# A gated mix of linear attention and a token-mixing MLP: the first loads in one queue

## The chip, the cores and the metric

One NeuronCore of a Trainium2 chip runs the whole kernel. The metric is the device time of one execution in microseconds (us), as the median of several runs; less is better. TensorE multiplies matrices (its weight loads are listed on their own, as PEld), VectorE (DVE) and ScalarE (ACT) work elementwise, GpSimd (POOL) has only some set-up here. Transfers are issued by an engine's queue, here SyncE's (SP) and in a few places ScalarE's (ACTq), and are carried out by 16 DMA engines.

## The reference

```python
def _B_ref(x, w1, b1, w2, b2):          # S=2048 tokens, D=512, F=1792
    h = _layernorm(x, axis=-1)
    u = jnp.einsum("bsd,sf->bdf", h, w1) + b1
    u = _gelu(u)
    y = jnp.einsum("bdf,fs->bds", u, w2) + b2
    return y.transpose(0, 2, 1)

def _A_ref(x, wqkv, wo):                # 32 heads of 16
    q, k, v = split(x @ wqkv)
    phi = lambda t: jnp.where(t > 0, t + 1, jnp.exp(t)) + 1e-6
    pq, pk = phi(q), phi(k)
    kv = jnp.einsum("bhsd,bhse->bhde", pk, v);  z = pk.sum(over tokens)
    o = (pq @ kv) / (pq . z + 1e-6)
    return o @ wo

g = _sigmoid((x * gate_w).sum(-1, keepdims=True))
out = g * _A_ref(x, ...) + (1 - g) * _B_ref(x, ...)
```

(Shapes and reshapes are shortened.) Two paths read the same x: linear attention, and an MLP that mixes over tokens, so that its first product sums over all 2048 tokens. A gate per token mixes the two.

## The kernel before

Tokens are cut into 16 tiles of 128 (t), D into 4 blocks, F into 14 blocks of 128 (j or f). TensorE's work stands in the program's order, in these stages:

1. 18 warm-up matmuls on constants (`warm_ps`).
2. `accA`: the first 8 blocks of u. For t = 0 to 11 all eight blocks are fed from token tile t (`mlp1(accA[j], w1A, j * P, t, ...)`), so the matmuls go t by t, eight at a time; the last four tiles go block by block, each followed by its gelu. A matmul of tile t needs `xh[:, t, :]`, the normalised tile, and block j of `w1A[:, t, :]`.
3. `kacc` and `Gps`: phi(k), and the product of pk with x.
4. `accB`, the last 6 blocks of u, mixed with `kvps`, `w2ps` and `qacc` (q and phi(q)).
5. `yps`: for each token tile 14 matmuls over f (`w2h` with `uT`) and 4 over attention (`pqT` with `W2sb`), in groups of tiles 0-7, 8-11, 12-14 and 15. In a group all f products come first, and the attention products of its tiles after them.

The layernorm of a tile is VectorE's and ScalarE's work: VectorE takes the statistics of x tile t (L195, tiles 1 and 3 in two halves), aggregates them (L198), ScalarE takes the square root (`sd`, L200), VectorE the reciprocal (L206) and applies it (`xh`, L208). VectorE runs its instructions strictly in the order written, which is: statistics and aggregate of tile 0, the first half of tile 1's statistics, reciprocal and `xh` of tile 0, the second half of tile 1, its aggregate, `xh` of tile 1, statistics of tile 2, and so on. At tile 8 it also turns `b_rows`, the bias rows, into columns (L234 to L236).

Transfers are issued by the helper `load` (L123), on SP unless another queue is named; every one of them has line 124 in the profile. `pin` keeps the written order. Before the change ScalarE's queue issues two of the first loads: b1's rows and the first 128 columns of w1's row tile 0 (L134, L135). SP issues x tile 0, x tile 1, the other 896 columns of w1's row tile 0, row tile 1, x tiles 2 and 3, and from there x tile t+1 and w1 row tile t in turn, b2's rows behind row tile 4 (L138 to L148). Then come the gate's row, wk, the 16 transposing loads of x, w1's last 768 columns (`w1B`), wv, wo and wq. Each transfer signals its end on one of eight semaphores, used in turn over both queues; a transfer is issued only when the one eight places before it has landed.

Late in the kernel SP also carries `w2`: its first half into the buffer of `w1A`, its second half into that of `w1B`, which comes free when the last accB matmul has run. The second half is issued in pieces (`pieces`, L508) between the stores of the normalised q tiles to DRAM (L414) and the transposing loads that bring them back as `pqT` (L416).

Of the kernel before, what the change touches and what calls it, by code (L numbers as in the profile page):

```python
# [15 lines left out]
def kernel(  # L16
# [13 lines left out]
    nc = tc.nc  # L30
    P = nc.NUM_PARTITIONS
# [11 lines left out]
    NF = F // P  # L43
# [4 lines left out]
    FA = NFA * P  # L48
# [5 lines left out]
    w1_view = B_w1.rearrange("(t p) f -> p t f", p=P)  # L54
    w2_view = B_w2.rearrange("(f p) s -> p f s", p=P)
    b1_view = B_b1.rearrange("(f p) -> f p", p=P)
# [9 lines left out]
    def ptile(shape, dt, name):  # L66
        return persist.tile(shape, dt, name=name, tag=name)
# [27 lines left out]
    b_rows = ptile([32, P], BF16, "b_rows")  # L95
# [22 lines left out]
    w1A = wpool.tile([P, NT, FA], BF16, name="w1A", tag="w1st")  # L118
# [4 lines left out]
    def load(o, i, eng=None, **kw):  # L123
        pin((eng or nc.sync).dma_start(out=o, in_=i, **kw))  # L124

    def load_x(t0, t1):
        load(xr[:, t0:t1, :], x_view[:, t0:t1, :])

    def load_w1a(t):
        load(w1A[:, t, :], w1_view[:, t, 0:FA])  # L130


    tbl = work.tile([P, 1], FP32, name="tbl", tag="tbl", bufs=2)
    load(b_rows[0:NF, :], b1_view, nc.scalar)  # L134
    load(w1A[:, 0, 0:P], w1_view[:, 0, 0:P], nc.scalar)  # L135
    pin(nc.scalar.activation(out=tbl[:], in_=eps_t[:], func=ACT.Sqrt))

    load_x(0, 1)  # L138
    load_x(1, 2)
    load(w1A[:, 0, P:FA], w1_view[:, 0, P:FA])  # L140
    load_w1a(1)
    load_x(2, 3)
    for t in range(2, NT):
        if t + 1 < NT:
            load_x(t + 1, t + 2)
        load_w1a(t)
        if t == 4:
            load(b_rows[NF : NF + NT, :], b2_view)  # L148
    load(gw_b[:], gw_row_view.to_broadcast([P, D]))
    load(wk_sb[:], wqkv_view[:, :, D : 2 * D])  # L150
# [354 lines left out]

    pieces = {0: ((0, 4), (4, 7)), 5: ((7, 9),), 7: ((9, NF),)}  # L508
    for t in range(12):
        normalise(t)  # L510
        if t % 4 == 3:
# [83 lines left out]
```

## Time and profile before

| | us |
|---|---|
| median of 3 runs | 163.27 (162.86 to 163.67) |
| the profiled execution | 163.07 |
| its span, first to last instruction | 161.4 |
| TensorE matmul busy | 157.6 (98%) |
| VectorE busy | 118.7 (74%) |
| ScalarE busy | 53.1 (33%) |
| moved by DMA | 28.33 MB, 176 GB/s on the mean |

The span is the profiler's, and it is shorter than the execution's own time by what lies before the first and after the last instruction. A slice of the page's second part is a fortieth of the span, some 4 us. The chain of waits is followed back from the last instruction, at each step to what released it; shares in it are what set the end, while shares of busy time are not. In rows of instructions the columns are start, duration, engine, line, operation, output from inputs, shape, count, and in square brackets the idle time before it with what ended it. A duration of an SPq or ACTq row is the time that the queue takes to issue the transfer, not the transfer.

### The profile page before, as it was taken

To read this page: it belongs to the slowest core of one execution; us is meant where nothing else is said; L and a number is where in the kernel's file an instruction comes from. 1 tells how busy PE (TensorE), PEld (TensorE's weight loads), DVE (VectorE), ACT (ScalarE), POOL (GpSimd) and SP (SyncE) were. 2 spreads that over 40 slices of the span, in tenths; PEclk is the share of its full clock that TensorE was granted. 3 is DMA by queue.
4 is the path that set the end of the run, shared out by engine and by line. 5 is a ranking of instruction groups with operands and counts; after the bars stand their busy time and mean duration, and the time that the engine had idled before them with its cause. 6 is when DMAs were issued, how large, how long until landed. Compare 5 with 4: busy or idle time off the path is not lost.

```text
span 161.4 us, 2274 instructions
## 1 busy us (share of the span) xinstructions
PE 157.6 (98%) x820; PEld 73.1 (45%) x820; DVE 118.7 (74%) x278; ACT 53.1 (33%) x89; POOL 1.2 (1%) x8
## 2 busy tenths in 40 slices
PE   7999999999999999999999999999999999999993
PEld 5444444444444444444444444444444444444452
DVE  2799998959999998899895999999999970000002
ACT  4122227794342321434225970000008300550050
POOL 2000000000000000000000000000000000000000
PEclk9999999999999999999999999999999999999999
DMA  4999999444699630229952007826525935744421
GB/s 124 308 342 351 341 283 149 108 103 106 158 391 391 149 123 0 87 50 300 399 214 67 0 33 262 290 66 154 174 65 124 340 89 126 230 143 100 151 98 33
DMA packets 36838, 28.33 MB, mean 176 GB/s; under 512 B 20444, under 2 KB 31196, under 8 KB 36828
## 3 DMA queue, kind: packets, MB, share of 16 engines
q1 hardware_dynamic: 36384, 27.90, 57.6%
q10 hardware_dynamic: 444, 0.30, 0.6%
q8 instruction: 6, 0.10, 0.3%
q14 instruction: 4, 0.03, 0.0%
HBM read 19.28 MB, written 4.46 MB: 147 GB/s over the span
## 4 chain that ended last, share of the span: by engine, by line
PE 95%; DMA 2%; ACTq 0%; DVE 0%; issue 0%; DVEq 0%
PE yps L74 39%; PE accA L74 17%; PE accB L74 13%; PE qacc L74 9%; PE Gps L74 9%; PE kacc L74 9%; DMA w1A<-in_B_w_dram 2%; ACTq L124 0%; PE kvps L74 0%; DVE ot L539 0%; PE w2ps L74 0%; DVE b_rows L114 0%; DVEq L539 0%; DVE eps_t L115 0%
## 5 line engine op out<-in xcount | busy, mean ns | idle before, releaser
L74 PE MATMUL yps<-uT,w2h 128*128 128x512 bf16 (+2 forms) x238 | 49.2, 366 | 0.0
L74 PEld LDWEIGHTS <-w2h 128*128 128x128 bf16 x238 | 22.8, 98 | 25.9
L74 PE MATMUL accA<-xh,w1A 128*128 128x512 bf16 x128 | 28.0, 381 | 0.1
L532 ACT ACTIVATE ot<-yps,c,c 128x512 bf16<-128x512 f32 x15 | 11.6, 777 | 46.9 <-PE yps L74 34.8
L74 PE MATMUL accB<-xh,w1B 128*128 128x512 bf16 x96 | 21.5, 379 | 0.0
L539 DVE TENSOR_SCALAR ot<-yps,c,c 128x384 bf16<-128x384 f32 (+1 forms) x2 | 1.1, 542 | 25.5 <-PE yps L74 25.5
L74 PEld LDWEIGHTS <-w1A 128*128 128x128 bf16 x128 | 12.6, 98 | 15.6 <-DMA w1A<-in_B_w_dram 0.6
L74 PEld LDWEIGHTS <-xT 128*128 128x128 bf16 x128 | 12.3, 98 | 14.9 <-issue 0.2
L74 PE MATMUL Gps<-pk,xr 128*128 128x512 bf16 x64 | 15.8, 379 | 0.0
L74 PE MATMUL kacc<-wk_sb,xT 128*128 128x512 bf16 x64 | 15.8, 379 | 0.0
L74 PE MATMUL yps<-W2sb,pqT 128*128 128x512 bf16 (+2 forms) x68 | 14.6, 366 | 0.0
L74 PEld LDWEIGHTS <-w1B 128*128 128x128 bf16 x96 | 9.4, 98 | 11.3
L74 PE MATMUL qacc<-wq_sb,xT 128*128 128x512 bf16 x64 | 14.5, 379 | 0.0
L288 ACT ACTIVATE e<-qacc 128x512 bf16<-128x512 f32 x16 | 9.6, 597 | 12.2 <-DVE kvbdT L436 4.6
L288 ACT ACTIVATE e<-kacc 128x512 bf16<-128x512 f32 x16 | 9.2, 598 | 12.7 <-DVE pk L295 6.8
L290 DVE TENSOR_SCALAR e<-e 128x512 bf16<-128x512 bf16 x32 | 9.2, 288 | 4.6 <-ACT e L288 4.3
L195 DVE BATCH_NORM_STATS2 stats<-xr 128x6 f32<-128x512 bf16 (+1 forms) x18 | 10.9, 608 | 2.1 <-DMA xr<-in_A_x_dram 2.1
L408 DVE SCALAR_TENSOR_TENSOR pq<-pq,odds,rd 128x512 bf16<-128x512 bf16 x16 | 12.0, 752 | 0.6
L404 DVE TENSOR_REDUCE den<-prod 128x32 f32<-128x544 f32 x16 | 11.5, 720 | 0.6
L295 DVE SCALAR_TENSOR_TENSOR pk<-kacc,e 128x512 bf16<-128x512 f32 x16 | 11.1, 692 | 1.0
L295 DVE SCALAR_TENSOR_TENSOR pq<-qacc,e 128x512 bf16<-128x512 f32 x16 | 11.1, 692 | 0.6
L247 DVE CUSTOM_DVE_ANT_0 junk<-xr,gw_b 128x512 bf16<-128x512 bf16 x16 | 11.0, 690 | 0.5
(52 smaller groups left out, 95.5 us busy)
## 6 DMA issues: line engine op xcount, KB each, us to landing
w1A<-in_B_w_dram SPq DMA_DIRECT2D x15, 256.0 KB, 4.1
w2h<-in_B_w_dram SPq DMA_DIRECT2D x2, 1792.0 KB, 9.6
w1B<-in_B_w_dram SPq DMA_DIRECT2D x4, 768.0 KB, 7.6
xr<-in_A_x_dram SPq DMA_DIRECT2D x16, 128.0 KB, 4.0
q_dram<-pq SPq DMA_DIRECT2D x16, 128.0 KB, 3.4
out_dram<-ot SPq DMA_DIRECT2D x15, 128.0 KB, 1.9
w2h<-in_B_w_dram SPq DMA_DIRECT2D x1, 1280.0 KB, 6.7
w2h<-in_B_w_dram SPq DMA_DIRECT2D x1, 1024.0 KB, 5.1
```

Of the source, the lines that this page charges most:

```text
L74: nc.tensor.matmul(o, lhsT=lhsT, rhs=rhs, start=start, stop=stop, **kw)
L195: pin(nc.vector.bn_stats(out=stats[t][:, h, :], in_=xr[:, t, d0:d1]))
L247: nc.vector.tensor_tensor_reduce(out=junk[:], in0=xr[:, t, :], in1=gw_b[:], scale=1.0, scalar=0.0, op0=ALU.mult, op1=ALU.add, accum_out=gp ...
L288: pin(nc.scalar.activation(out=e[:], in_=acc[:], func=ACT.Exp))
L290: nc.vector.tensor_scalar(out=e[:], in0=e[:], scalar1=1.0, scalar2=PHI_EPS, op0=ALU.min, op1=ALU.add)
L295: nc.vector.scalar_tensor_tensor(out=o, in0=acc[:], scalar=0.0, in1=e[:], op0=ALU.max, op1=ALU.add)
L404: pin(nc.vector.tensor_reduce(out=den[:], in_=prod[:], op=ALU.add, axis=AX.X))
L408: nc.vector.scalar_tensor_tensor(out=heads, in0=heads, scalar=odds[:, t : t + 1], in1=rd[:].unsqueeze(2).to_broadcast([P, NH, HEAD]), op0= ...
L532: nc.scalar.activation(out=ot[:, d0:d1], in_=yps[:, d0:d1], func=ACT.Identity, scale=c1[:, t : t + 1], bias=c2[:, t : t + 1],)
L539: nc.vector.tensor_scalar(out=ot[:, d0:d1], in0=yps[:, d0:d1], scalar1=c1[:, t : t + 1], scalar2=c2[:, t : t + 1], op0=ALU.mult, op1=ALU.add,)
```

## The change

The two loads of ScalarE's queue move to SP's. The first 128 columns of w1's row tile 0 are issued between x tile 0 and x tile 1; the other 896 columns are split into columns 128 to 512 (blocks 1 to 3) and 512 to 1024 (blocks 4 to 7); b1's rows are issued in front of b2's, behind w1's row tile 4. In the late part, the first seven blocks of w2's second half are issued as one transfer instead of two. No computing instruction changes, and their order on TensorE, VectorE and GpSimd stays the same.

```diff
     tbl = work.tile([P, 1], FP32, name="tbl", tag="tbl", bufs=2)
-    load(b_rows[0:NF, :], b1_view, nc.scalar)
-    load(w1A[:, 0, 0:P], w1_view[:, 0, 0:P], nc.scalar)
     pin(nc.scalar.activation(out=tbl[:], in_=eps_t[:], func=ACT.Sqrt))
 
     load_x(0, 1)
+    load(w1A[:, 0, 0:P], w1_view[:, 0, 0:P])
     load_x(1, 2)
-    load(w1A[:, 0, P:FA], w1_view[:, 0, P:FA])
+    for f0, f1 in ((P, FA // 2), (FA // 2, FA)):
+        load(w1A[:, 0, f0:f1], w1_view[:, 0, f0:f1])
     load_w1a(1)
     load_x(2, 3)
     for t in range(2, NT):
         if t + 1 < NT:
             load_x(t + 1, t + 2)
         load_w1a(t)
         if t == 4:
+            load(b_rows[0:NF, :], b1_view)
             load(b_rows[NF : NF + NT, :], b2_view)
...
-    pieces = {0: ((0, 4), (4, 7)), 5: ((7, 9),), 7: ((9, NF),)}
+    pieces = {0: ((0, 7),), 5: ((7, 9),), 7: ((9, NF),)}
```

## The prediction

> **What bounds the kernel now.** The page comes first: which engine is busy in which slice, then the chain of waits.
>
> ```profile
> PE   7999999999999999999999999999999999999993
> PEclk9999999999999999999999999999999999999999
> PE 95%; DMA 2%; ACTq 0%; DVE 0%; issue 0%; DVEq 0%
> ```
>
> TensorE is busy in every slice at the full granted clock, and the chain that ended last is TensorE for 95%. Only 2% (3.26 us) of it is a transfer. The chain in order of time says which one:
>
> ```profile
> 1.02 0.63 ACTq L124
> 1.69 3.26 DMA w1A<-in_B_w_dram
> 4.99 28.02 PE accA L74 x128
> ```
>
> Columns are start, length, what. ScalarE's queue issues b1's rows (0.63), then w1's first 128 columns (issued at 1.69, landed 4.94), and TensorE's real work starts at 4.99. From there it hardly pauses: 128 accA matmuls take 28.02, where the steady pitch of 0.216 would take 127 x 0.216 = 27.4 plus the last one. A change to the loads can therefore move the end only through the first microseconds, or by making a later wait that is not there now. The timeline of the start:
>
> ```profile
> 0.80 0.87 SPq L124 DMA_DIRECT2D xr<-in_A_x_dram  x2
> 1.72 0.91 SPq L124 DMA_DIRECT2D w1A<-in_B_w_dram  x2
> 2.67 0.91 SPq L124 DMA_DIRECT2D xr<-in_A_x_dram  x2
> 3.65 0.18 DVE L198 BATCH_NORM_AGGREGATE mv<-stats 128x2 f32<-128x6 f32 x1
> 3.75 0.39 DVE L195 BATCH_NORM_STATS2 stats<-xr 128x6 f32<-128x256 bf16 x1
> 4.39 0.41 DVE L208 TENSOR_SCALAR xh<-xr,mv,rstd 128x512 bf16<-128x512 bf16 x1
> 6.55 0.69 DVE L195 BATCH_NORM_STATS2 stats<-xr 128x6 f32<-128x512 bf16 x1 [0.19 <-DMA xr<-in_A_x_dram]
> 8.02 0.41 DVE L208 TENSOR_SCALAR xh<-xr,mv,rstd 128x512 bf16<-128x512 bf16 x1
> ```
>
> Xh0, the first right-hand operand, is ready at 4.39 + 0.41 = 4.80, so w1's first block at 4.94 is what TensorE waits for. VectorE, working strictly in order, then waits 0.19 us for x tile 2 (6.55). That makes xh2 ready at 8.02 + 0.41 = 8.43. TensorE's weight loads show a second, smaller loss:
>
> ```profile
> 4.99 0.98 PEld L74 LDWEIGHTS <-w1A 128*128 128x128 bf16 x5 [0.63 <-DMA w1A<-in_B_w_dram]
> ```
>
> By the single matmuls, the first three begin at 4.99, 5.39 and 5.65, where two pitches are 0.43 and not 0.66: the second block waits for the rest of w1's row tile 0 (landed 5.16). Then tile t=1 begins at 6.94, t=2 at 8.67, t=3 at 10.40. Their operands are ready at 6.36 (xh1), 8.43 (xh2), 10.08 (xh3, 9.67 + 0.41): slacks of 0.58, 0.24 and 0.32, and 0.86 or more from t=4 on.
>
> **The change, part by part.** *Removed from ScalarE's queue:* two issues, 0.63 + 0.39. ScalarE's next duty on the path is sd of tile 0 at 3.87, behind a table load that ends at 3.38; it gets earlier, but VectorE's row (aggregate end 3.83) decides, so this is worth nothing.
>
> *w1's first block on SP.* SP's issues follow each other every 0.475 us (1.72, 2.20, 2.67, 3.15 in the trace). The block is issued at about 1.26 instead of 1.69 and lands by 1.26 + 2.1 (x tiles 0 and 1 from issue to landing) to 1.26 + 3.26 (its own time now), so between 3.4 and 4.5. Either is before xh0's 4.80 and the end of the warm-up matmuls (4.42 + 0.42 = 4.84). TensorE then starts at 4.87 or so: gain 0.12.
>
> *Blocks 1-3 and 4-7 apart.* Issued at about 2.2 and 2.7; with the 3.4 us that the one piece takes now, they land at 5.6 and 6.1 at worst, with 2.1 us at 4.3 and 4.8. Needed at 4.87 + 0.22 = 5.1 and 5.74. I take values near 4.7 and 5.0, since less is in the queue ahead of them than a full row, and so the 0.23 us lost between the first three matmuls goes too. Together at most -0.35.
>
> *x tile 1 moves behind the block.* Its issue goes from 1.26 to 1.73 and its landing from 3.33 to about 3.80 (latency 2.07 kept). VectorE wants it at 3.75, in front of rstd and xh0, which stand behind it on the in-order engine; rstd waits for sd until 4.17 anyway, and the half statistics take 0.39. Cost 0 to 0.05; if it lands 0.3 later, xh0 and TensorE's start are later by 0.3 and the gain is gone.
>
> *x tile 2 is the step that decides.* It stands behind two more SP issues: 2.67 becomes about 3.6. It took 3.85 us from issue to landing, against 2.1 for tile 0, so most of that was queueing at the DMA engines, whose share is 0.8 to 1.0 from 1.8 us on:
>
> ```profile
> 1.80:2.50 0.70, 0.70 (x6) 0.46 (x3) 0.00 (x0) 0.40 (x1) 0.05 (x1) 1.00 0.79 216
> 2.50:3.50 1.00, 1.00 (x6) 0.75 (x5) 0.58 (x1) 0.99 (x2) 0.00 (x0) 1.00 0.79 191
> 3.50:4.50 1.00, 1.00 (x7) 0.61 (x5) 0.88 (x5) 0.40 (x2) 0.00 (x0) 1.00 0.89 304
> 4.50:5.50 1.00, 0.85 (x4) 0.32 (x3) 0.85 (x3) 0.08 (x1) 0.00 (x0) 1.00 0.96 285
> ```
>
> (The last three columns are granted clock, DMA share, GB/s.) The same bytes stand ahead of tile 2 in both kernels, so if the engines were never short of work it would land when it does now. If the landing follows the issue, it is later by 0.95. Call the delay of its landing d: from -0.4 (in this trace three of its packets took 0.9 us each, which need not fall there again) to +0.95. I take +0.15, near the queueing end, with a little lost because SP supplies about 128 KB per issue of 0.475 us (some 270 GB/s) while the pieces are small. Xh2 is then ready at 8.43 + d, and TensorE's t=2 begins at 8.43 + d + 0.05, or 0.35 earlier than now, whichever is later. Against 8.67 that is **max(-0.35, d - 0.19)**: -0.04 at d = 0.15, -0.35 at best, +0.76 at d = 0.95. Tile 3's operand follows 1.65 behind xh2 (10.08 - 8.43) and TensorE's tile takes 1.73, so nothing is added there.
>
> [...] Row: the first block took 3.26 us on ScalarE's queue, while SP's x tiles took 2.1, and its data moved between theirs. [...]
>
> *b1's rows behind tile 4.* Some 0.4 us more on SP, ahead of x tile 6 and everything later, 1.3 with the two above. The transposes of b_rows run at 14.80, and b2's rows, issued at 6.07, landed by 9.87. Later x tiles: VectorE has 0.86 us in hand at t=4 and 1.4 at t=15 (xh15 ready 25.14, needed 26.59), w1 row tiles 1.0 us and more from tile 2 on (landed 7.66, needed 8.67). The DMA engines run at about 345 to 380 GB/s from 6.5 to 10.5, so the lost issue time is filled from what is queued. Cost 0; with the cover gone, up to 0.4. The x transposes and wk come by 27.8, needed at 33.0.
>
> *w2's second half, first seven blocks in one transfer.* One SP issue less at 96.4, same bytes. Two pieces landed at 103.86, 7.5 us after the first issue; a single seven-block transfer of w2's first half took 7.6 from issue, and the one behind it 4.5 after that. So +0.1 at worst, -3 at best. What stands behind it is a chain: q stores, four transposes (to 110.0), the stores of tiles 4 to 7, four transposes (to 122.2), then w2's last five blocks, issued 122.26 and landed 128.95. Tile t=8 needs block 9 at 127.04 + 9 x 0.216 = 128.98: 0.03 us in hand. A delay there is passed on in full, an advance brings nothing. I take 0; bounds 0 and +0.1.
>
> **Sum.** Profiled execution 163.07 (span 161.4 and 1.67 around it): -0.04 + 0 + 0 = 163.03. The median shown is 0.20 above that execution, so about 163.2 against 163.27. Bounds of the sum: -0.35 and +0.76 + 0.4 + 0.1 = +1.26.
>
> **The rivals.**
> - *Gain realised (162.9).* x tile 2 lands no later than now, or sooner without the long packets: -0.20 to -0.35. For it: DMA share near full, same bytes. Against: SP's supply is no more than what the engines take.
> - *Slower: x tile 2 follows its issue (164.0).* It lands 0.95 later, VectorE waits 1.1 instead of 0.19, TensorE stands still before t=2: 163.27 + 0.76 = 164.0. It makes the kernel slower from d = 0.19 on and by over 0.8 us from d = 1.0. For it: tiles 0 and 1 landed just 2.1 after their issue, that is, they followed it. Against: tiles 2 and 3 took 3.85 and 3.69, so they queued.
> - *w2's merged piece delays the last five blocks (163.4 to 164).* Price: whatever it lands later than 103.86, less 0.03. For it: the slack of 0.03. Against: same bytes, and the 7.6 us row.
> - *It doesn't do what it says (163.3).* The instruction order of the changed kernel shows both loads on SP and VectorE's and TensorE's order untouched, so what could fail is the effect: the first block, now inside SP's stream, lands as late as 4.9.
>
> **How the numbers follow.** Forecast (within 0.25 of now) 0.56; gain realised 0.20; slower by x tile 2 0.14; w2's piece 0.06; no effect at the start 0.04. A change of 0.5% is 0.82 us, about what a measurement of this kernel can tell from no change (its three runs span 0.81). No working gives a gain over 0.35, so a faster verdict needs the measurement's own spread or delays in the runs that the profiled one lacks: 0.06. A slower one needs the upper part of the second and third rival: 0.11. Within: 0.83. Range: -0.35 and +0.76 about 163.27, widened by some 0.2 to 0.4 for the spread of the runs: 162.5 to 164.1.
>
> **What would show it.** First block: TensorE's first accA at 4.85 to 4.90, no wait put down to w1A, the next two 0.216 apart. x tile 1: VectorE's half statistics still at 3.75 to 3.85. x tile 2: the wait of VectorE for xr, 0.19 now, is 0.19 + d, and a pause of TensorE of 0.1 to 0.3 appears before its 17th accA. Late part: no wait of TensorE in yps. I am wrong if the first accA begins after 5.0, if TensorE pauses over 0.8 us before t=3, or if yps shows a pause.

## The result and the profile after

The changed kernel takes 163.64 us (median of 22 runs, 163.13 to 164.18), the kernel before 163.12 (22 runs beside them, 162.67 to 163.67): a ratio of 1.0034, 95% interval 1.0022 to 1.0046. It is slower by about 0.5 us, where 0.07 us less was forecast. Ratios leave out executions over 1.5% above a kernel's fastest, which are two of `two_more`'s twelve (340 and 431 us) and three of `x1_third_b`'s twelve (165.7 us, a time that half of `x1_third`'s six runs also took). The profiled execution has a span of 162.3 against 161.4.

Of the page's fourth part, the chain by engine, one line of the changed kernel:

```profile
PE 68%; DVE 17%; DMA 8%; SPq 4%; issue 1%; ACT 0%; DVEq 0%
```

TensorE alone made 95% of it before; now VectorE, transfers and SP's issues stand in it too. Most of that is the late part, where the chain leaves TensorE at 86.66 and runs through VectorE's work on q, the q stores and SP's issues to w2's last blocks at 130.10. The chain in order of time (start, length, what) begins so:

```profile
0.79 0.40 SPq L124
1.26 0.41 SPq L124
1.72 2.62 DMA xr<-in_A_x_dram
4.36 0.43 DVE stats L196
4.89 0.42 DVE xh L209
5.35 7.37 PE accA L74 x31
```

What starts TensorE is no longer w1's first block but x tile 1, issued third on SP (1.72), landed at 4.34. The same moments in the timeline:

```profile
4.36 0.43 DVE L196 BATCH_NORM_STATS2 stats<-xr 128x6 f32<-128x256 bf16 x1 [0.56 <-DMA xr<-in_A_x_dram]
5.35 6.93 PE L74 MATMUL accA<-xh,w1A 128*128 128x512 bf16 x29 [0.52 <-DVE xh L209]
7.04 0.69 DVE L196 BATCH_NORM_STATS2 stats<-xr 128x6 f32<-128x512 bf16 x1 [0.18 <-DMA xr<-in_A_x_dram]
8.51 0.41 DVE L209 TENSOR_SCALAR xh<-xr,mv,rstd 128x512 bf16<-128x512 bf16 x1
```

VectorE waits 0.56 us for x tile 1, in front of xh0, where it did not wait at all; TensorE's first accA begins at 5.35 instead of 4.99. The wait for x tile 2 is still 0.18, but it ends at 7.04 instead of 6.55, and xh2 is ready at 8.92 instead of 8.43. The weight loads of the first matmuls:

```profile
5.36 0.10 PEld L74 LDWEIGHTS <-w1A 128*128 128x128 bf16 x1 [0.80 <-DMA w1A<-in_B_w_dram]
5.73 0.15 PEld L74 LDWEIGHTS <-w1A 128*128 128x128 bf16 x1 [0.27 <-issue]
6.16 0.15 PEld L74 LDWEIGHTS <-w1A 128*128 128x128 bf16 x1 [0.28 <-issue]
6.51 5.49 PEld L74 LDWEIGHTS <-w1A 128*128 128x128 bf16 x26 [0.21 <-issue]
```

All of w1's row tile 0 had landed by 4.99, and still the first pitches are 0.38, 0.43 and 0.35 before the steady 0.216. The idle time before the second to fourth of these loads ends in "issue", not in a transfer.

Kacc's weight loads start 0.65 later than before (33.28 against 32.63): 0.36 is the later start and 0.28 the slow pitches (0.51 over the steady three against 0.23). The other 0.32 of the span's 0.97 is a pause of TensorE's matmuls in tile 8 of yps, where w2's last five blocks landed at 130.10 (the idle time in the row, 0.63, is that of the weight loads, which start 0.21 ahead of their matmuls here):

```profile
130.14 0.76 PEld L74 LDWEIGHTS <-w2h 128*128 128x128 bf16 x5 [0.63 <-DMA w2h<-in_B_w_dram]
```

One execution shows 0.97 where the medians differ by 0.52, so not all of these pieces belong to the change. Nor does this execution wait at t=2: its slow pitches bring TensorE there at 9.32, when both operands are in (xh2 at 8.92, w1's row tile 2 at 8.75). The experiments had to say which pieces belong to the change.

### The profile page after: what moved, and what is told of

It reads as the page before. It is cut to its first block, busy times and chain, and to the rows that moved or that the text cites. A ratio compares the mean times of both kernels' runs of the same rounds, so it can differ in the third digit from the quotient of the medians.

```text
span 162.3 us, 2261 instructions
## 1 busy us (share of the span) xinstructions
PE 157.3 (97%) x806; PEld 73.0 (45%) x820; DVE 118.9 (73%) x278; ACT 53.0 (33%) x89; POOL 1.2 (1%) x8
## 4 chain that ended last, share of the span: by engine, by line
PE 68%; DVE 17%; DMA 8%; SPq 4%; issue 1%; ACT 0%; DVEq 0%
PE yps L74 18%; PE accA L74 17%; PE kacc L74 9%; PE accB L74 8%; PE Gps L74 8%; PE qacc L74 6%; DMA w2h<-in_B_w_dram 4%; DVE den L405 4%; DVE pq L409 4%; SPq L124 4%; DVE prod L400 3%; DMA q_dram<-pq 2%; DVE pq L296 2%; DVE rd L407 2%; DMA xr<-in_A_x_dram 2%
```

## The experiments

Ratios are to the kernel before, run on the same chip beside each group, with 95% intervals. Landing times are those of a transfer's last part, from the trace. "Slot" means one SP issue, 0.475 us.

### First group: undoing one part

x tile 1 back in its place (`x1_first`):

```diff
 load_x(0, 1)
+load_x(1, 2)
 load(w1A[:, 0, 0:P], w1_view[:, 0, 0:P])
-load_x(1, 2)
```

> The changed kernel with x tile 1 issued again right behind x tile 0 and w1's first block third. Theory (x tile 1's place): tile 1 lands near 3.3 as before, VectorE does not wait for it, xh0 is ready at 4.80 and the first accA begins at 4.85 to 4.90 instead of 5.35. x tile 2 still lands near 7.0, so TensorE pauses before t=2 until about 8.97, and of the 0.65 us by which kacc came later some 0.3 to 0.4 are won back: ratio to the kernel before 1.000 to 1.002. Rival (the merged piece of w2): the time stays at 1.003, because the end is set late. Rival (w1's small pieces are what is slow): the first accA is still at 5.2 or later.

1.0025 (1.0008 to 1.0041). VectorE no longer waits for tile 1 and the first accA begins at 4.90, as the theory had it. The rest of it failed: x tile 2 landed at 6.31 and not near 7.0, no pause came before t=2 (five slow pitches had TensorE there only at 9.30), and the ratio missed the 1.000 to 1.002 expected. Only a quarter of the loss goes, and the interval includes that none does.

The late part undone (`late_undone`):

```diff
-pieces = {0: ((0, 7),), 5: ((7, 9),), 7: ((9, NF),)}
+pieces = {0: ((0, 4), (4, 7)), 5: ((7, 9),), 7: ((9, NF),)}
```

> The changed kernel with w2's first seven blocks again in two pieces; the start stays as changed. Theory (the start sets it): first accA at 5.3 to 5.4, kacc's start 0.5 to 0.65 later than in the kernel before, ratio 1.003 as in the full change. Rival (the merged piece of w2 delays the last five blocks): the pause of TensorE at the tenth f block of tile 8 goes, and the ratio falls to 1.000 to 1.001.

1.0038 (1.0023 to 1.0053): w2's merged piece is not what costs the 0.5 us. Kacc's start is another matter: it is 0.12 later than before and not 0.5 to 0.65, because the first pitches are all 0.216 here. The weight loads of this run:

```profile
5.09 3.12 PEld L74 LDWEIGHTS <-w1A 128*128 128x128 bf16 x15 [0.84 <-DMA w1A<-in_B_w_dram]
8.77 0.11 PEld L74 LDWEIGHTS <-w1A 128*128 128x128 bf16 x2 [0.57 <-DMA w1A<-in_B_w_dram]
```

Without slow pitches TensorE would begin tile t=2 at 8.53 and begins it at 8.78, when its weights are in. Xh2 was ready at 8.49; w1's row tile 2 landed at 8.73 (7.66 in the kernel before). This pause is the first sight of the change's main cost.

b1's rows alone moved, the rest as before (`b1_alone`):

```diff
-load(b_rows[0:NF, :], b1_view, nc.scalar)
...
         if t == 4:
+            load(b_rows[0:NF, :], b1_view)
             load(b_rows[NF : NF + NT, :], b2_view)
```

> The kernel before with one part of the change alone: b1's rows move to SP behind w1's row tile 4; w1's first block stays on ScalarE's queue, now first in it, and row tile 0's rest stays one piece. Theory: w1's first block is issued at 0.8 instead of 1.69 and lands by 3.5, x tiles 1 and 2 land as before (3.3, 6.5), the first accA begins at 4.85 to 4.90, TensorE's t=2 waits for xh2 until 8.47, so kacc begins about 0.2 us sooner than before: ratio 0.998 to 1.000. Rival (any two issues at once hurt the x tiles): x tile 0 or 1 lands later than now and the ratio is above 1.000.

1.0012 (0.9998 to 1.0026). The hoped-for start at 4.87 failed: with w1's first block issued at 0.79, in the same moment as x tile 0, tile 0 landed at 3.06 instead of 2.90, and accA began at 5.02. In the three profiles in which ScalarE's queue issues a part of w1 by 1.03, x tile 0 landed at 3.04 to 3.37, in the other sixteen at 2.87 to 3.00.

Four more warm-up matmuls in the changed kernel (`warm22`):

```diff
-    for _ in range(18):
+    for _ in range(22):
```

> The changed kernel with 22 instead of 18 warm-up matmuls, which then last until about 5.27 instead of 4.83, so that TensorE hardly idles before the first accA at 5.35. Theory W (the first accA matmuls are slow because the array still runs at half rate after the idle time): the first three pitches fall from 0.38, 0.43 and 0.35 to 0.22 or one of them stays high, and kacc begins 0.2 to 0.35 sooner than in the changed kernel. Rival (they wait for data, or the array's rate follows a clock of its own): the pitches stay, and kacc begins where it did, 33.6, or up to 0.1 later.

1.0052 (1.0030 to 1.0073), slower. Its weight loads:

```profile
4.21 0.74 PEld L74 LDWEIGHTS <-const-bfloat16-1.0 128*128 128x128 bf16 x5
4.97 3.23 PEld L74 LDWEIGHTS <-w1A 128*128 128x128 bf16 x16
```

All accA pitches up to t=2 are 0.216, but four warm-ups already ran at 0.113 instead of 0.213, from 4.6 on, so TensorE changed its rate while it was busy and not because the idle time was filled. late_undone changed its rate during the warm-ups too, from 3.9 on, then idled 0.67 us and was fast from its first accA. So theory W in this form falls: idle time before accA is not the cause.

### Second group: which part alone reproduces the loss

The late part alone (`merge_alone`):

> The kernel before with the late part of the change alone: w2's first seven blocks of the second half in one transfer. Theory (the start is what costs): ratio 0.9995 to 1.0005, since the same bytes land within 0.1 us of the same moment. Rival (the merged piece costs): w2's last five blocks land after the tenth f block of tile 8 wants them, TensorE pauses there by 0.3 to 0.5 us, ratio 1.002 to 1.003.

The diff is the last line of the change. 1.0002 (0.9985 to 1.0019): no measurable cost. Its profile does show a pause at w2's last blocks (0.38 us of the matmuls), so the slack of 0.03 is sometimes overrun; over the twelve runs no loss is clear. It also settles the first pitches, as the rest of row tile 0 had landed at 4.92:

```profile
5.26 0.15 PEld L74 LDWEIGHTS <-w1A 128*128 128x128 bf16 x1 [0.20 <-issue]
5.69 0.15 PEld L74 LDWEIGHTS <-w1A 128*128 128x128 bf16 x1 [0.27 <-issue]
6.12 2.92 PEld L74 LDWEIGHTS <-w1A 128*128 128x128 bf16 x14 [0.28 <-issue]
```

The pitches behind 5.26 are 0.427 with the data there: twice the steady one (0.216), and twice the 0.213 that a warm-up of half the columns takes.

Two issues added to the kernel before, nothing else (`two_more`):

```diff
     load(w1A[:, 0, P:FA], w1_view[:, 0, P:FA])
+    for spare in (ptile([NT, P], BF16, "spare0"), ptile([NT, P], BF16, "spare1")):
+        load(spare[:], b2_view)
     load_w1a(1)
```

> The kernel before with two more small loads on SP (b2's rows, 4 KB each, into tiles that nothing reads) behind the rest of w1's row tile 0, so ahead of w1's row tile 1 and x tiles 2 and 3; ScalarE's two loads, x tile 1 and all else as before. Theory S (the two more issues on SP make x tiles 2 and 3 late): x tile 2 is issued at 3.4 to 3.6 and x tile 3 at 3.9 to 4.1 and lands at 7.4 or later; xh2, behind tile 3's first half in VectorE's order, is ready 0.1 to 0.5 later than 8.43; first accA at 4.9 to 5.0 as before; ratio 1.001 to 1.003. Rival (x tile 1's place alone does it): no more than 1.000.

1.0027 (1.0008 to 1.0046). Most of the change's loss comes with two small loads ahead of w1's row tile 1, with x tile 1, both queues and w2 as before. x tile 2 landed at 6.72 and w1's row tile 2 at 8.62, and VectorE's wait for x tile 2 is twice the 0.19 of before:

```profile
6.74 0.69 DVE L197 BATCH_NORM_STATS2 stats<-xr 128x6 f32<-128x512 bf16 x1 [0.39 <-DMA xr<-in_A_x_dram]
```

This execution does not wait at t=2 either: four slow pitches bring TensorE there at 9.08, behind both operands (xh2 at 8.65).

x tiles 2 and 3 pulled forward in the changed kernel (`x23_early`; arguments shortened, and the loop no longer loads x tile 3):

```diff
-for f0, f1 in ((P, FA // 2), (FA // 2, FA)):
-    load(w1A[:, 0, f0:f1], ...)
+load(w1A[:, 0, P : FA // 2], ...)
+load_x(2, 3)
+load(w1A[:, 0, FA // 2 : FA], ...)
+load_x(3, 4)
 load_w1a(1)
-load_x(2, 3)
```

> The changed kernel, same loads and same number, with x tile 2 issued in front of blocks 4-7 and x tile 3 in front of w1's row tile 1; x tile 1 stays behind w1's first block. Theory S: x tile 2 lands near 6.0 and x tile 3 near 6.8, xh2 is ready by 8.45 and TensorE does not pause before t=2; what is left is x tile 1, by which the first accA begins at 5.0 to 5.3; ratio 1.001 to 1.002, against 1.0034. Rival (x tile 1 alone): ratio stays at 1.003 or more. Rival (w1 now comes too late): a wait for w1A before t=1.

And with x tile 1 in front (`x123_early`):

> The same with x tile 1 also back behind x tile 0, so that the order is x 0, x 1, w1 block 0, blocks 1-3, x 2, blocks 4-7, x 3, w1's row tile 1. Theory (x tiles 1 to 3 are what the change made late): first accA at 4.85 to 4.90, xh2 by 8.4, no pause before t=2 over 0.1; ratio 0.998 to 1.000. Rival (the loads in small pieces or the longer SP queue cost by themselves): ratio 1.002 or more.

1.0065 (1.0041 to 1.0089) and 1.0033 (1.0012 to 1.0053). The forecast failed in both, by the rival named with the first: w1's row tile 1 became the wait. It was issued at 4.09 and 4.08, landed at 8.02 and 7.83, and TensorE stood before t=1. In the first:

```profile
8.06 1.25 PE L74 MATMUL accA<-xh,w1A 128*128 128x512 bf16 x5 [1.23 <-DMA w1A<-in_B_w_dram]
```

The x tiles came early there (5.38 and 6.03). Neither of these two orders serves all: what is issued sooner puts something else back. The two differ in x tile 1's place alone and by 0.0032, at the edge of what their intervals can tell.

### Third group: the dose, and x tile 1 alone

Three small loads instead of two (`three_more`):

> The kernel before with three small loads more on SP ahead of w1's row tile 1 and x tiles 2 and 3 (two gave 1.0027). Theory S (what is issued later lands later and TensorE waits for xh2): x tile 2 is issued at 4.1 or when the first block has landed, x tile 3 half a microsecond behind, xh2 is ready at 8.9 to 9.4, ratio 1.004 to 1.007, more than with two. Rival (the two loads cost by something else, such as their packets): about as with two.

The edit is that of two_more, with three loads: 1.0051 (1.0031 to 1.0071). The timeline shows the waits and the pause:

```profile
6.79 0.69 DVE L198 BATCH_NORM_STATS2 stats<-xr 128x6 f32<-128x512 bf16 x1 [0.40 <-DMA xr<-in_A_x_dram]
8.61 0.41 DVE L211 TENSOR_SCALAR xh<-xr,mv,rstd 128x512 bf16<-128x512 bf16 x1
9.21 0.60 PE L74 MATMUL accA<-xh,w1A 128*128 128x512 bf16 x2 [0.53 <-DMA w1A<-in_B_w_dram]
```

Xh2 is ready at 9.02, w1's row tile 2 landed at 9.16, and t=2 begins at 9.21. Both operands are late, the weights by a little more. The small loads, 4 KB each, are work of their own for the DMA engines, so these runs alone do not tell an issue's time from the work of a small transfer; the changed kernel adds no bytes.

x tile 1 third on SP, with w1's 896 columns on ScalarE's queue so that SP has no slot more than before (`x1_third`, then `b0_third`):

```diff
-load(w1A[:, 0, 0:P], w1_view[:, 0, 0:P], nc.scalar)
+load(w1A[:, 0, P:FA], w1_view[:, 0, P:FA], nc.scalar)
...
 load_x(0, 1)
+load(w1A[:, 0, 0:P], w1_view[:, 0, 0:P])
 load_x(1, 2)
-load(w1A[:, 0, P:FA], w1_view[:, 0, P:FA])
```

> The kernel before with only x tile 1's place changed: on SP x tile 0, w1's first block, x tile 1, w1's row tile 1, x tiles 2 and 3 (these three issued at 2.2, 2.7, 3.15 as before); the 896 other columns of w1's row tile 0 take the first block's place on ScalarE's queue, behind b1's rows. Theory: x tile 1 lands at 3.8 to 4.3 and VectorE waits 0.05 to 0.5 for it; the first accA begins at 4.9 to 5.3; x tiles 2 and 3 land as before (about 6.2 and 6.9), xh2 at 8.2 to 8.5. Ratio 1.0005 to 1.0015, the smaller part of the change's 1.0034. Rival (x tile 1 is the whole loss): 1.003.

> The same with x tile 1 back behind x tile 0 and w1's first block third on SP: no issue more on SP ahead of w1's row tile 1 than before, first block no longer behind b1's rows. Theory: first accA at 4.85 to 4.95, xh2 by 8.4, ratio 0.998 to 1.0005. Rival (any change of the first loads' order costs): ratio above 1.001.

1.0106 (1.0065 to 1.0146) and 0.9987 (0.9971 to 1.0003). In the first, the 896 columns were issued at 1.67, just ahead of x tile 1 (1.72), which then landed at 5.27:

```profile
5.29 0.43 DVE L195 BATCH_NORM_STATS2 stats<-xr 128x6 f32<-128x256 bf16 x1 [1.47 <-DMA xr<-in_A_x_dram]
5.81 0.41 DVE L208 TENSOR_SCALAR xh<-xr,mv,rstd 128x512 bf16<-128x512 bf16 x1
6.28 3.40 PE L74 MATMUL accA<-xh,w1A 128*128 128x512 bf16 x15 [1.44 <-DVE xh L208]
```

So a late x tile 1 does hold back xh0, which does not need it, through VectorE's order, and what stands ahead of it matters. As a measure of x tile 1's place in the change the run fails, since 224 KB stood there that the change doesn't put there. Its six runs lie in two groups, three at 163.9 to 164.1 and three at 165.6 to 165.7; the profile is of the first group, and what the second waits for is not known. b0_third has the lowest ratio of all, but its interval includes 1.

VectorE's order changed in the changed kernel (`if t == 2` becomes `if t in (2, 3)`; `x3_behind`):

> The changed kernel with VectorE's order changed at one place: the statistics of x tile 3 are taken whole and behind reciprocal and xh of tile 2, instead of their first half in front. Theory (xh2 waits for x tile 3, which stands in front of it): xh2 is ready 0.65 behind x tile 2's aggregate whenever tile 3 lands, 0.1 to 0.4 sooner; xh3 comes up to 0.4 later, and TensorE's t=3 is then close to waiting; ratio 1.0015 to 1.003 instead of 1.0034. Rival (x tile 2's landing or x tile 1 alone sets it): 1.003 to 1.004, unchanged.

1.0033 (1.0018 to 1.0047): unchanged. x tile 2 landed at 6.96 and xh2 was ready at 8.87 with tile 3 out of its way, only 0.05 sooner than in the changed kernel, whose profile shows no wait of VectorE for x tile 3 at all. xh3 came late instead: TensorE lost 0.18 us before t=3. That VectorE's order at x tile 3 is the main cost falls.

### Last two groups: one slot, and the change's own parts undone

One small load (`one_more`):

> The kernel before with one small load more (b2's rows into a tile that nothing reads) on SP ahead of w1's row tile 1 and x tiles 2 and 3. Theory S (each issue ahead of x tile 2 makes it later, of which TensorE feels what is over its slack): ratio 1.0005 to 1.002, between 1.000 and the 1.0027 of two. Rival (the slack takes one issue whole): 0.9995 to 1.0005.

1.0003 (0.9987 to 1.0020): the value is the rival's, by which the slack takes one slot, but the interval holds both forecasts.

The pair that differs in x tile 1's place alone, with the 896 columns and both bias rows behind the table load on ScalarE's queue (`x1_third_b`, then `b0_third_b`):

> The kernel before with, on SP, x tile 0, w1's first block, x tile 1, w1's row tile 1, x tiles 2 and 3 (from row tile 1 on at the same times as before); on ScalarE's queue, behind the first table load, w1's 896 other columns, b1's and b2's rows. So x tile 1 is one issue later, with 32 KB and not 256 KB ahead of it. Theory (x tile 1's place costs what VectorE then waits): x tile 1 lands at 3.8 to 4.2, VectorE waits 0.05 to 0.4, first accA at 4.9 to 5.2, xh2 by 8.5; ratio 1.000 to 1.0015, and 0.0005 to 0.0015 above b0_third_b. Rival (x tile 1's place is most of the change's loss): 1.0025 or more.

> The same with x tile 1 ahead of w1's first block. Theory: x tile 1 lands at 3.35, the first block at 3.7 and the 896 columns at 5.0 to 5.2, first accA at 4.85 to 4.90, xh2 at 8.2 to 8.4; ratio 0.998 to 1.000, a gain of 0 to 0.3 us. Rival (the 896 columns, issued 0.6 later than before, become the wait): TensorE waits for w1A behind its first accA, 5.2 or later, and the ratio is 1.000 to 1.001.

1.0012 (0.9994 to 1.0030) and 1.0007 (0.9990 to 1.0025). First accA at 5.59 and 5.00; the ratios are 0.0005 apart, less than either interval. Three of x1_third_b's twelve runs took 165.7, as half of x1_third's did, and none of b0_third_b's; with them x1_third_b's mean is 1.005 of the kernel before. The pair is not as clean as meant: the 896 columns did not stay behind the table load (below) and were issued at 1.03, so x tile 1 landed later in both, at 4.57 and 3.96.

w1's 896 columns in one piece again in the changed kernel (`unsplit`), and the same with x tile 1 back (`unsplit_x1`):

```diff
-for f0, f1 in ((P, FA // 2), (FA // 2, FA)):
-    load(w1A[:, 0, f0:f1], w1_view[:, 0, f0:f1])
+load(w1A[:, 0, P:FA], w1_view[:, 0, P:FA])
```

> The changed kernel with w1's 896 columns in one piece again, so that one issue and not two is added on SP ahead of w1's row tile 1 and x tiles 2 and 3; x tile 1 stays behind w1's first block. Theory S with slack for one issue: x tile 2 is issued at 3.1, xh2 is ready by 8.6, and what is left is x tile 1's place: ratio 1.0003 to 1.0018. Rival (the number of issues is not it): 1.003 or more.

> The same with x tile 1 back behind x tile 0. Theory: first accA at 4.85 to 4.95, x tile 2 issued at 3.1, ratio 0.999 to 1.001. Rival: 1.002 or more.

1.0016 (1.0001 to 1.0030) and 1.0018 (1.0006 to 1.0030). Taking one of the two slots back about halves the loss, though the intervals touch; x tile 1's place then adds nothing. The second was expected within 0.001 of the kernel before and is above it: its profile has x tile 2 in at 7.03, fifteen of its sixteen parts by 6.08, so one late part set it there.

Put in order of slots, with the time at which both operands of t=2 were there in the profile (the later of xh2 and w1's row tile 2; for one_more xh2). Left out are x1_third, x1_third_b, x23_early and x123_early, in which something in front of t=2 was late, x tile 1 or w1's row tile 1:

| slots more ahead of x tile 2 | kernel: operands of t=2 ready | ratios |
|---|---|---|
| 0 | before 8.43, merge_alone 8.18, b1_alone 8.32, b0_third 8.19, b0_third_b 8.29 | 1, 1.0002, 1.0012, 0.9987, 1.0007 |
| 1 | one_more 8.73, unsplit 8.43, unsplit_x1 8.94 | 1.0003, 1.0016, 1.0018 |
| 2 | after 8.92, two_more 8.65, x1_first 8.81, late_undone 8.73, x3_behind 8.87, warm22 9.09 | 1.0034, 1.0027, 1.0025, 1.0038, 1.0033, 1.0052 |
| 3 | three_more 9.16 | 1.0051 |

The means of the middle column are 8.28, 8.70, 8.85 and 9.16.

How this becomes time can be read from the profiles. From t=2 to kacc's first weight load they all take 23.96 us (x3_behind 0.18 more), so the start of t=2 carries the whole difference of the first part. It begins at the later of two moments: the operands', and TensorE's own arrival, which is the first accA, 16 pitches of 0.216 (3.46 us) and what its slow pitches add, 0 to 0.95 us from profile to profile. The spread of the runs fits that: the kernel before takes 162.67 to 163.67, and late operands lift the lowest times first, by 0.25 (one_more), 0.66 (two_more) and 1.08 us (three_more, whose six runs lie within 0.37 us) over the lowest of the kernel before beside them. This is a reading of spreads; no run here sets the number of slow pitches.

## Why the prediction was wrong

**What bounds the start** was read rightly: only the first microseconds, or a new wait, could move the end.

**The step that failed is x tile 2's, `max(-0.35, d - 0.19)`, put at -0.04, together with w1's row tiles at "Cost 0".** It is the cost of two slots on SP, and it was mis-sized in all three of its terms. d, x tile 2's delay, was taken as 0.15 and was 0.49 in the profiled pair (6.53 to 7.02). Over the profiles with two slots more x tile 2 landed at 6.67 on the mean (6.31 to 7.02), over the five of the table's first row at 6.12 (5.91 to 6.53): a delay of 0.55, and the one profile that the prediction had was the latest of its kind. The argument that the DMA engines queue anyway, so the landing would hardly move, was too strong. Second, w1's row tile 2 came 1.1 later in the pair (7.66 to 8.75), 0.93 on the means of the same profiles. The prediction covered that tile with "1.0 us and more" of slack, which is just what the two slots use up. Third, the slack of 0.24 before t=2 was a matter of one execution: 0.23 of it are the two slow pitches of the first matmuls (4.99 + 3.46 + 0.23 = 8.67). At full rate TensorE arrives at 8.45, 0.02 behind xh2, and a delay is passed on nearly whole.

The dose by small loads agrees: one slot 1.0003, two 1.0027, three 1.0051. From the second on a slot costs about 0.0024 of 163 us, 0.39 us, most of its 0.475. The second rival had the nearest mechanism, though not the whole size (+0.52 measured, +0.76 priced) and not the whole path: where TensorE is seen to stand still before t=2, it is w1's row tile 2 that came last in late_undone, warm22 and three_more, and xh2 in x3_behind and unsplit_x1.

**The gain of 0.35 had no ground.** Its larger part, "so the 0.23 us lost between the first three matmuls goes too", took the slow pitches for a wait for w1. They are TensorE at half rate, 0.427 against 0.216 in merge_alone: they appear with all the data landed (after, merge_alone) and are absent in late_undone and x3_behind. How many there are, none to five, differs between executions: the steady pitch began at 3.9, among the warm-ups, in late_undone and at 6.93 in x1_first. Without it the step's bound is 0.12 and not 0.35.

Of its own signs of being wrong two came in the changed kernel's profile, the first accA after 5.0 (5.35) and a pause in yps (0.32). By the runs neither is the main cost.

**x tile 1**, costed at 0 to 0.05, made VectorE wait 0.56 in the changed kernel's profile and 0.02 to 0.28 in the five others that have its place and its loads around it (late_undone, warm22, x23_early, x3_behind, unsplit). The mechanism was named, the size was ten times too small in the first. In time it shows as 0.0009 (after less x1_first), 0.0005 (x1_third_b less b0_third_b, without the runs at 165.7), -0.0002 (unsplit less unsplit_x1) and 0.0032 (x23_early less x123_early, with another order behind it): in the changed kernel no part of it is clear of the intervals. A reason offers itself, which no run isolates: what TensorE loses at the start it saves before t=2 where the later operands set that.

**b1's rows and w2's merged piece** at nothing: for the merged piece merge_alone says the same, within 0.0017 either way. b1's share was not separated in the runs, as b1_alone (1.0012) moves the block's issue as well; but from t=2 to kacc the changed kernel's profile takes the same 23.96 us as the one before, so b1's rows cost nothing there.

**The issue time** that ScalarE's queue kept off SP is what the change gave away: ahead of x tile 2 one of the two slots of 0.475 us, w1's first block; the other comes from splitting the 896 columns. By one_more, unsplit and unsplit_x1 one slot is worth 1.0003 to 1.0018, by two_more both are worth 1.0027.

What stays open: the 0.0015 of the ratio of unsplit_x1 over one_more, both with one slot more, which their intervals can explain; x tile 1's share; the runs at 165.6 to 165.8 of x1_third and x1_third_b; and the pause at w2's last blocks. Matmuls lost 0.12 to 0.49 us by it in four of the nine profiles with the merged piece (after, warm22, merge_alone, x23_early) and nothing in the ten without it. That the merged piece makes the pause likelier is probable by this count. On the mean of the nine it would be 0.14 us, 0.0009 of the time, which the intervals of merge_alone and late_undone cannot tell from nothing.

## What to carry to other kernels

At the start, one queue's issue slots, 0.475 us each here, are a resource of their own: count how many stand ahead of each transfer, and compare the sum with the slack of everything behind them, weights as well as inputs. A slack about equal to the delay is no cover. Before a slow stretch of an engine is put down to a transfer, look whether the transfer had landed and whether the pitch in it is twice the steady one, as 0.427 against 0.216 here. A slack read from one execution can be made of such a stretch, so compare several. And "needed later" is decided by the order of the engine that reads it: a tile that is needed second can hold back the first, by 1.42 us in x1_third (xh0 ready at 6.22 and not 4.80).

## What the hardware showed that was not expected

TensorE's rate doubles at a moment that differs between executions with the same first matmuls. Warm-up matmuls of 256 columns follow each other every 0.213 us and accA matmuls of 512 columns every 0.427, until a moment between 3.5 (x23_early and b0_third_b, among the warm-ups) and 6.9 us (x1_first); then every 0.113 and 0.216. The profile's windows print a granted clock of 1.00 for every stretch from 0 to 9.5 of the changed kernel, where the steady pitch begins at 6.51, so the doubling does not show in that column; the trace's own record of the clock starts only at 6.43 there, and at 5.47 in the kernel before. The moments lie 3.4 us apart over the profiles, and no run here shows what sets them.

ScalarE's queue issued transfers ahead of an instruction that stands before them. In x1_third_b the table load and an activation are written first, but:

```profile
0.80 1.28 ACT L134 ACT_TABLE_LOAD   x1 [0.80 <-PEq L578]
1.03 0.40 ACTq L124 DMA_DIRECT2D w1A<-in_B_w_dram  x1
2.09 0.20 ACT L134 ACTIVATE tbl<-eps_t 128x1 f32<-128x1 f32 x1
```

The transfer was issued at 1.03, while the table load ran until 2.08; b0_third_b did the same at the same time. In these two runs the written order on that engine did not hold the transfer back.
